# Gated linear attention and a gated expert on one core: smaller tiles on TensorE, decays loaded once, and new constants for the planner

## The chip, the cores and the metric

The kernel runs on one core of one Trainium2 chip. The time is the device time of one execution in microseconds (us); three executions of the kernel before were timed, and one more was profiled.

## The reference

For each of 4 batches and 8 heads, a state of 48 x 48 numbers is carried over 768 steps; its result, reshaped to 3072 tokens of 384 values, goes through a normalised, gated expert. All is float32.

```python
B, H, S, D = 4, 8, 768, 48
for t in range(S):
    state = alpha[:, :, t, :, None] * state + einsum('bhd,bhe->bhde', k[:, :, t], v[:, :, t])
    y[:, :, t] = einsum('bhd,bhde->bhe', q[:, :, t], state)
x  = y as (3072, 384)
xn = x / sqrt(mean(x * x) + 1e-6) * rms_g
g, val = xn @ w_gate, xn @ w_val            # (384, 1536) each
out = (g * sigmoid(g) * val) @ w_out        # (1536, 384)
```

## The kernel before

**Chunks.** The sequence is cut into 24 chunks of 128 steps (6 per batch; c0 to c3 are the first chunk of each batch, c4 to c7 the second, and so on). Eight heads make four pairs: the two heads of a pair lie on partitions 0 to 47 and 64 to 111. Products are kept near float32 by writing each operand as a high and a low f16 half and adding three products (`SPLIT`): high x high, high x low, low x high.

**Attention of a chunk** (`attention`, one operation after the other): SyncE (SP) loads `att`, 112 rows that hold four segments of decays (back half turned, front half, back half, front half turned), then q and k. VectorE (DVE) runs one scan over two segments (`scan`, L601), takes reciprocals of its ends into `seed2` (`turn`, L606), runs a second scan over the other two, and multiplies k and q by the products of decays (`mul_k` L616, `mul_q` L621). Both scans write in place, over the decays in `att`. ScalarE (ACT) copies the ends of the first scan into `dec` (`ends`, L609). Then come f16 halves of k, q and v (ACT the high, DVE the low), the scores on TensorE (PE) (`scores`, L691), the mask (L704), f16 halves of the masked scores (L755, L758), and the output `y` (`output`). For each pair of heads `output` makes six matmuls of q with the state (L772: stationary 48 x 128, 48 moving columns) and six of the scores with v (L781: stationary 128 x 128, 48 moving columns). `sums` (L798: stationary 64 x 64 or 64 x 48, 48 moving columns, 48 matmuls a chunk) renews the state. For c0 to c3 scores and output are float32 matmuls (L699, L731). After that the norm makes `x16` (L850, L854, L857), and a transposing DMA writes it to `xT`.

**Expert.** The chunks form groups of 4, 2, 2, 4, 4, 4, 4. For each group, `expert_in` makes for 12 blocks f of the hidden size two sets of nine matmuls (L982) of 512 or 256 columns, then `silu` (L993), `gate` (L999), the high f16 half (L478) and the low one (L1012); `expert_out` makes the output matmuls (L1052). On PE the expert matmuls are chained in a fixed order: group 0 in, group 0 out, group 1 in, and so on; attention is placed between them. In group 0 the first `EARLY` = 3 blocks f are run on two chunks at a time (256 columns), the others on four.

**Weights.** 18 blocks (i0 to i11, o0 to o5) are loaded as 64-bit words and decoded by DVE: `shift` L520, `sign` L523, `rest` L528, and a low half (`low`, L536). For the names in `LOW_W` PE and ACT make the low half instead: an identity matmul in float32 (`bring`, L541), one that subtracts the high half (`less`, L548), and a copy by ACT (`residue`, L554).

**Order.** All operations go to a planner (`Plan.order`). Each has a cost, a due time worked back from its group's planned time (`PACE`, `GAP`, `AHEAD`, `STRIDE`, `FIRST_DUE`), and a shift by kind (`LATE`). The planner plays the engines through in time and, among operations that could start, takes the one that is due first; the instructions are then written to each engine in that order, and each engine runs them in that order whatever happens. `BUFS` says how many buffers a name has; `att` has three.

**Verdict.** At the end `verdict` squares and sums statistics and sets a flag that picks a slow general path if a value was out of bounds. One matmul there (L1188) sums 411 columns over the partitions, and DVE adds them up (L1190).

Of the kernel before, what the change touches and what calls it, by code (L numbers as in the profile page):

```python
# [8 lines left out]
F32 = mybir.dt.float32  # L9
# [3 lines left out]
ALU = mybir.AluOpType  # L13
# [15 lines left out]
SPLIT = ((0, 0), (0, 1), (1, 0))  # L29
# [12 lines left out]


GROUPS = [4, 2, 2, 4, 4, 4, 4]
EARLY = 3


OUT32 = 4
LOW_A = ()
LOW_H = ()  # L50
LOW_W = ("i0", "i1", "i2", "i3")

BUFS = dict(
    att=3, v=2, kh=2, qp=2, k16=2, q16=2, kT=2, v16=4, gd=2, a16=2, ss=2, x32=1, x16=2,
    xT=2, raw=2, wu=2, h16=13, sl=2, h32=3, ob=2, at=3, y=1, mm=3,
)

# [4 lines left out]
    abs=0.92, wh=0.83, pow=0.65, sc=0.8, sc32=2.3, y=0.87, y0=0.5, y32=1.85, u=0.45, po=1.48,  # L62
    neg=0.3, wid=1.6, wneg=0.45, wl2=0.85,
)
IN_COST = {
# [4 lines left out]
LOAD_LAG, LOAD_END, LOAD_RATE = 0.6, 0.9, 230.0  # L70


PACE = [1.0, 1.0, 1.15, 1.18, 1.18, 1.18, 1.18]
GAP = [0, 14, 0, 0, 0, 0, 0]
FIRST_DUE = [-14.0, -8.0, -2.0, 4.0]
AHEAD = [0, 4, 8, 12, 16, 16, 16]
STRIDE = [0, 8, 12, 12, 20, 20, 20]
LATE = dict(load=0.0)
CUTS = [0, 2, 4]
SIDE = [3, 1]  # L80

# [1 line left out]
class Plan:  # L83
# [6 lines left out]
        self.users = {}  # L90
        self.slot = {}

    def op(self, engine, cost, fn, deps=(), use=(), due=None, lock=False, kb=0, late=0.0):

        o = dict(e=engine, c=cost, fn=fn, d=[d for d in deps if d], u=tuple(use), due=due, lock=lock,
                 kb=kb, late=late, i=len(self.ops), n=[])
        for d in o["d"]:
            d["n"].append(o)
        for k in o["u"]:
            self.users[k] = self.users.get(k, 0) + 1  # L100
        self.ops.append(o)
        return o

    def order(self):
# [8 lines left out]
        engine = dict.fromkeys(("PE", "DVE", "ACT", "POOL", "SP"), 0.0)  # L113
        ready = {e: [] for e in engine}
        wait = {o["i"]: len(o["d"]) for o in self.ops}
        for o in self.ops:
            o["r"] = 0.0
            if not o["d"]:
                ready[o["e"]].append(o)
        bus, port, done = 0.0, 0.0, []  # L120
# [209 lines left out]
def tile_attn_moe(  # L330
# [42 lines left out]
    raw_in = {}  # L373
    HC = C // 2
    SEG = NP * (HC + 1)
    o_a = 2 * SEG
    o_q = 4 * SEG
    o_k = o_q + NP * C

    def src(cc):  # L380
# [108 lines left out]
    def add(engine, kind, *args, **kw):  # L489
        return op(engine, COST[kind], *args, late=LATE.get(kind, 0.0), **kw)  # L490

    def decode(src, dst, name, col):
# [63 lines left out]
            )  # L556

        raw, wu = ("raw", name), ("wu", name)
        o = op("SP", 0.9, load, [], [raw], kb=786, late=LATE["load"])
# [20 lines left out]
    def attention(cc, due):  # L580
# [6 lines left out]
        def key(tag):  # L587
            return tag, cc
# [4 lines left out]
        def by_half(x):  # L593
            return x.rearrange("r p (g c) -> r g p c", g=2)

        def wseg():
            return att_tile(cc)[:, :o_q].rearrange("r (g p c) -> r g p c", g=4, p=NP)

        def scan(lo, start):
            x = att_tile(cc)[:, lo : lo + o_a]  # L600
            nc.vector.tensor_tensor_scan(  # L601
                x, x, start.rearrange("r g p c -> r (g p c)"), 0.0, op0=ALU.mult, op1=ALU.add
            )

        def turn():
            nc.vector.reciprocal(seed2[:, :, :, 0:1], wseg()[:, 2:4, :, HC : HC + 1])  # L606

        def ends():
            nc.scalar.copy(dec[:, cc], wseg()[:, 2:4, :, HC])  # L609
# [3 lines left out]
        def mul_k():  # L613
            t["kh"] = tl(ap, [R, NP, C], F32, "kh")
            k = att_tile(cc)[:, o_k:].rearrange(halves, p=NP, g=2)
            nc.vector.tensor_tensor(by_half(t["kh"]), k, wseg()[:, 0:4:3, :, :HC], op=ALU.mult)  # L616

        def mul_q():
            t["qp"] = tl(ap, [R, NP, C], F32, "qp")
            q = att_tile(cc)[:, o_q:o_k].rearrange(halves, p=NP, g=2)  # L620
            nc.vector.tensor_tensor(by_half(t["qp"]), q, wseg()[:, 1:3, :, 1:], op=ALU.mult)  # L621

        def k_hi():
            t["k16"] = tl(ap, [R, 2, NP, C], F16, "k16")
# [34 lines left out]
        def decay():  # L659

            t["gd"] = tl(ap, [R, NP, 1], F32, "gd")
            nc.vector.scalar_tensor_tensor(
                t["gd"][:, :, 0],
                dec[:, cc, 1],
                S_QP / (S_Q[1] * S_K[0]) * S_T / (S_K[1] * S_V),
                dec[:, cc - NB, 0],
                op0=ALU.mult,
                op1=ALU.mult,
            )
# [81 lines left out]
        def a_tile():  # L751
            return tile_of(("a16", cc), lambda: tl(ap, [P, 2, 2, NP, C], F16, "a16"))
# [9 lines left out]
        def output(h):  # L762
            if h == 0:
                t["y"] = tl(ps_y, [P, 2, 512], F32, "y")
            yps = t["y"]
            for p in (2 * h, 2 * h + 1):
                cs = slice(p * D, (p + 1) * D)
                if not first:
                    for m, (x, y) in enumerate(SPLIT):
                        for j in range(2):  # L770
                            r = slice(64 * j, 64 * j + D)
                            nc.tensor.matmul(  # L772
                                yps[:, j, cs],
                                t["q16"][r, x, p, :],
                                states[b][2][r, y, p, :],
                                start=m == 0,
                                stop=False,
                            )
                for j in range(2):
                    for m, (x, y) in enumerate(SPLIT):  # L780
                        nc.tensor.matmul(  # L781
                            yps[:, j, cs],
                            a_tile()[:, j, x, p, :],
                            t["v16"][:, y, j, p, :],
                            start=first and m == 0,
                            stop=m == 2,
                        )
# [78 lines left out]
        def x_turn():  # L866
# [4 lines left out]
                transpose=True,  # L871
            )

        att_k, at0, at1 = key("att"), ("at", (cc, 0)), ("at", (cc, 1))
        cuts = ((o_a, o_q), (0, o_a), (o_q, AW)) if cc < 2 else ((0, AW),)
        la = [
            op("SP", 0.45, lambda lo=lo, hi=hi: load_att(cc, lo, hi), use=[att_k], kb=(hi - lo) * R / 250)
            for lo, hi in cuts
        ]
        lv = op("SP", 0.45, lambda: load_v(cc), use=[key("v")], kb=196)  # L880
# [4 lines left out]
        s1 = add("DVE", "scan", lambda: scan(o_a, seed), [la[0]], [att_k], lock=True)  # L885
        rec = add("DVE", "rec", turn, [s1, prev.get("s2")], [att_k])
        de = add("ACT", "dec", ends, [s1], [att_k])
        s2 = add("DVE", "scan", lambda: scan(0, seed2), [rec, la[1 % len(la)]], [att_k], lock=True)
        kh = add("DVE", "kh", mul_k, [s2, la[-1]], [att_k, key("kh")], lock=True)
        qp = add("DVE", "kh", mul_q, [s2, la[-1]], [att_k, key("qp")], lock=True)  # L890
# [248 lines left out]
    def verdict():  # L1139
# [5 lines left out]
        def piece(rows, n):  # L1145
            used[0] += n
            return work[:rows, used[0] - n : used[0]]

        ones, sq, ok = piece(P, 1), piece(P, NS), piece(P, nok)
# [40 lines left out]
        nc.vector.tensor_reduce(  # L1190
            tot[:, 0:1], pok, axis=mybir.AxisListType.X, op=ALU.add
        )
        nc.vector.tensor_scalar(
            tot[:, 1:2],
            tot[:, 0:1],
# [35 lines left out]
def layout(inputs):  # L1231
# [8 lines left out]
    def pairs(x, pad):  # L1240
# [58 lines left out]
```

## Time and profile before

| | us |
|---|---|
| timed, median of 3 | 560.13 |
| timed, lowest and highest | 559.03, 560.67 |
| profiled execution | 559.45 |
| its span | 557.7 |
| PE busy in the span | 522.6 |
| DVE busy | 402.9 |
| ACT busy | 237.6 |

The profiled execution lies 0.68 us below the median and takes 1.75 us more than its span. Busy time is the time in which an engine had an instruction running. Matmuls overlap, so a busy PE may still do its work faster or slower; for a run of matmuls the distance from its first start to the start of what follows says more than the durations. The engines work at different loads in different stretches, so the shares over the whole span say little about what one change is worth.

### The profile page before, as it was taken

The page shows a single profiled execution, that of the slowest core. Times are in us where ns is not written, and L with a number is a line of the kernel's source. Part 1 is how long each engine was busy: PE and PEld are TensorE (multiplying, and loading weights), DVE is VectorE, ACT ScalarE, POOL GpSimd, SP SyncE. Part 2 cuts the span into 40 slices and gives each one's busy share as a digit, 9 for nine tenths or more (in the row PEclk, how much of TensorE's full clock was granted, in tenths as well). Part 3 has the DMA queues.
Part 4 walks back from the last instruction along what each step waited for, and adds up shares of the span by engine and source line. Part 5 has one row for each costly group of instructions (what it writes and reads, how often), then busy time and mean ns, then how long its engine had stood idle before and what let it go on. Part 6 is the DMA issues. An engine that isn't in the chain of part 4 may idle for free.

```text
span 557.7 us, 12089 instructions
## 1 busy us (share of the span) xinstructions
PE 522.6 (94%) x4986; PEld 309.0 (55%) x4986; DVE 402.9 (72%) x727; ACT 237.6 (43%) x636; POOL 22.1 (4%) x53
## 2 busy tenths in 40 slices
PE   2878899898999999999999999999999999999995
PEld 1756644355786787554556555456554456544452
DVE  7999999999996999787785687784577642133303
ACT  2446666755343665255542345542356431132300
POOL 2001000001000000000000010000000000000000
PEclk9986999989999999999999999999999999999998
DMA  8997875563822872334235233332211001000001
GB/s 221 298 303 151 259 199 168 170 179 62 222 68 48 176 176 70 72 90 102 48 81 128 75 82 99 46 82 61 74 29 18 15 15 45 28 1 0 1 29 34
DMA packets 59695, 56.15 MB, mean 101 GB/s; under 512 B 39472, under 2 KB 54960, under 8 KB 57168
## 3 DMA queue, kind: packets, MB, share of 16 engines
q1 hardware_dynamic: 59632, 55.30, 38.7%
q8 instruction: 41, 0.67, 0.5%
q14 instruction: 22, 0.18, 0.1%
HBM read 41.26 MB, written 4.72 MB: 82 GB/s over the span
## 4 chain that ended last, share of the span: by engine, by line
PE 79%; DVE 14%; DMA 4%; issue 2%; ACT 1%; SPq 0%; DVEq 0%
PE mm L982 47%; PE mm_po L1052 22%; PE y L781 3%; PE at L691 2%; PE y L772 2%; DMA rg<-rms_g 2%; DVE att L601 1%; PE at L798 1%; DVE wu_i L523 1%; DVE wu_o L523 1%; DVE wu_o L528 1%; DMA att<-att 1%; DMA kT<-k 1%; DVE wo L536 1%; DVE h L1012 1%
## 5 line engine op out<-in xcount | busy, mean ns | idle before, releaser
L982 PE MATMUL mm<-xT,wg 128*128 128x512 f16 (+1 forms) x1566 | 290.2, 344 | 3.4 <-ACT sl L993 1.6
L982 PEld LDWEIGHTS <-wg 128*128 128x128 f16 x1566 | 151.3, 98 | 127.1 <-issue 3.1
L1052 PE MATMUL mm_po<-wo,h 128*128 128x384 f16 x864 | 147.1, 328 | 5.8 <-DVE h L999 2.7
L1052 PEld LDWEIGHTS <-h 128*128 128x128 f16 x864 | 83.5, 98 | 63.0 <-issue 9.8
L478 ACT ACTIVATE h<-h 128x512 f16<-128x512 f32 (+1 forms) x87 | 48.2, 554 | 86.5 <-DVE h L999 86.0
L999 DVE SCALAR_TENSOR_TENSOR h<-mm,sl 128x512 f32<-128x512 f32 (+1 forms) x87 | 51.5, 592 | 41.6 <-PE mm L982 41.6
L1012 DVE TENSOR_TENSOR h<-h,h 128x512 f16<-128x512 f32 (+1 forms) x87 | 51.3, 591 | 20.9 <-ACT h L478 20.9
L601 DVE TENSOR_TENSOR_SCAN att<-att,seed 112x520 f32<-112x520 f32 x48 | 59.2, 1235 | 6.6 <-DMA att<-att 6.0
L993 ACT ACTIVATE sl<-mm 128x512 f32<-128x512 f32 (+1 forms) x87 | 45.1, 518 | 40.6 <-PE mm L982 40.0
L1063 DVE TENSOR_SCALAR ob<-mm_po 128x384 f32<-128x384 f32 x24 | 13.1, 551 | 33.4 <-PE mm_po L1052 33.3
L846 POOL TENSOR_TENSOR ss<-ss,mhalf 128x1 f32<-128x1 f32 x24 | 17.8, 740 | 444.4 <-DVE ss L836 408.7
L755 ACT CAST a<-at 128x512 f16<-128x512 f32 x40 | 23.2, 585 | 17.6 <-DVE at L704 17.4
L704 DVE TENSOR_TENSOR at<-at,mask 128x512 f32<-128x512 f32 x40 | 26.1, 692 | 4.1 <-PE at L691 4.0
L758 DVE TENSOR_TENSOR a<-at,a 128x512 f16<-128x512 f32 x40 | 25.9, 682 | 0.4
L781 PE MATMUL y<-v,a 128*128 128x48 f16 x480 | 25.7, 185 | 0.0
L830 ACT ACTIVATE junk<-y 128x384 bf16<-128x384 f32 x24 | 11.8, 490 | 31.0 <-DVE x L850 17.4
L478 ACT ACTIVATE v<-v 128x384 f16<-128x384 f32 x24 | 12.5, 519 | 26.2 <-PE at L798 23.9
L628 DVE TENSOR_TENSOR k<-kh,k 112x512 f16<-112x512 f32 x24 | 16.5, 686 | 9.6 <-ACT k L478 9.6
L478 ACT ACTIVATE k<-kh 112x512 f16<-112x512 f32 x24 | 15.0, 626 | 14.4 <-DMA kT<-k 9.9
L850 DVE TENSOR_TENSOR x<-y,rg 128x384 f32<-128x384 f32 x24 | 13.2, 552 | 9.9 <-PE y L781 8.4
L854 ACT ACTIVATE x<-x,ss 128x384 f16<-128x384 f32 x24 | 14.7, 611 | 13.4 <-POOL ss L846 12.6
L772 PE MATMUL y<-s,q 48*128 48x48 f16 x480 | 19.7, 184 | 0.0
(99 smaller groups left out, 426.7 us busy)
## 6 DMA issues: line engine op xcount, KB each, us to landing
att<-att SPq DMA_DIRECT2D x22, 903.0 KB, 5.8
v<-vtok SPq DMA_DIRECT2D x24, 192.0 KB, 2.8
raw_i<-w_gate SPq DMA_DIRECT2D x12, 384.0 KB, 4.0
raw_i<-w_val SPq DMA_DIRECT2D x12, 384.0 KB, 4.8
raw_o<-w_out SPq DMA_DIRECT2D x6, 768.0 KB, 4.5
out_dram<-ob SPq DMA_DIRECT2D x24, 192.0 KB, 2.1
att<-att SPq DMA_DIRECT2D x4, 227.5 KB, 4.1
att<-att SPq DMA_DIRECT2D x2, 448.0 KB, 7.4
```

The costliest lines, as they stand in the source:

```text
L478: nc.scalar.activation(dst, src, AF.Copy, scale=scale, accum_out=stat[:rows, col : col + 1])
L601: nc.vector.tensor_tensor_scan(x, x, start.rearrange("r g p c -> r (g p c)"), 0.0, op0=ALU.mult, op1=ALU.add)
L704: nc.vector.tensor_tensor(t["sc"][j], t["sc"][j], mask[:, int(first)].to_broadcast([P, NP, C]), op=ALU.mult,)
L755: nc.scalar.copy(a_tile()[:, j, 0], t["sc"][j])
L758: nc.vector.tensor_tensor(a_tile()[:, j, 1], t["sc"][j], a_tile()[:, j, 0], op=ALU.subtract)
L772: nc.tensor.matmul(yps[:, j, cs], t["q16"][r, x, p, :], states[b][2][r, y, p, :], start=m == 0, stop=False,)
L781: nc.tensor.matmul(yps[:, j, cs], a_tile()[:, j, x, p, :], t["v16"][:, y, j, p, :], start=first and m == 0, stop=m == 2,)
L982: nc.tensor.matmul(ps[:, :n], wg[:, f, x, j, kk, :], xT[:, y, kk, cs], start=i == 0, stop=i == 3 * NK - 1,)
L993: nc.scalar.activation(t["sl"][:, :n], t[0][:, :n], AF.Silu, scale=1.0 / (S_X * S_W))
L999: nc.vector.scalar_tensor_tensor(t["h"][:, :n], t[1][:, :n], S_H / (S_X * S_W), t["sl"][:, :n], op0=ALU.mult, op1=ALU.mult,)
L1012: nc.vector.tensor_tensor(h16_of(g, f)[:, 1, cs], t["h"][:, :n], h16_of(g, f)[:, 0, cs], op=ALU.subtract)
L1052: nc.tensor.matmul(t[i][:, :DM], h16_of(g, f)[:, x, ts], wo[:, f // 2, y, f % 2, :], start=f == 0 and m == 0, stop=f == NF - 1 and m == 2,)
```

## The change

- `att` now holds the decays once: back half, then front half reversed in time and in pair order, with one column more. The row falls from 2064 to 1545 numbers. The first scan reads the segment forward, the second reads the same numbers backward (a step of -1), and both write into a new tile `dk`, which has a single buffer. The reciprocals, `mul_k`, `mul_q` and `decay` read it with the pairs in reverse where needed. For c0 and c1 the load is cut in two parts and not three.
- `output` cuts each matmul in two: L772's into four tiles of 48 x 64 (two heads, two halves of the queries), L781's into two of 128 x 64. A chunk after c3 has 96 matmuls there and not 48. Columns, products and sums are the same.
- `verdict` adds along the columns on DVE first, and its last matmul has one column.
- `EARLY` is 5, `LOW_W` is i0, i1, o1, i11, i7.
- All constants of the planner's due times are new, `LATE` has an entry for most kinds, and `HOLD` gives times in the plan before which the loads of some chunks and weights are not taken. `HOLD` changes the order only; the engine does not wait for a time.

```diff
-EARLY = 3
+EARLY = 5
-LOW_W = ("i0", "i1", "i2", "i3")
+LOW_W = ['i0', 'i1', 'o1', 'i11', 'i7']
-    att=3, v=2, kh=2, qp=2, k16=2, q16=2, kT=2, v16=4, gd=2, a16=2, ss=2, x32=1, x16=2,
+    att=3, v=2, kh=2, qp=2, k16=2, q16=2, kT=2, v16=4, gd=2, a16=2, ss=2, dk=1, x32=1, x16=2,
-PACE = [1.0, 1.0, 1.15, 1.18, 1.18, 1.18, 1.18]
-GAP = [0, 14, 0, 0, 0, 0, 0]
-FIRST_DUE = [-14.0, -8.0, -2.0, 4.0]
-AHEAD = [0, 4, 8, 12, 16, 16, 16]
-STRIDE = [0, 8, 12, 12, 20, 20, 20]
-LATE = dict(load=0.0)
+PACE = [0.939, 1.309, 1.366, 1.325, 1.11, 1.095, 1.217, 1.519]
+GAP = [0, 9.2, -0.3, -0.8, 7.1, 0.3, 11.3, 10.4]
+FIRST_DUE = [-19.3, -19.1, -6.2, -12.5]
+AHEAD = [0, 6.1, 6.5, 12.3, 23.9, 15.3, 13.6, 8.2]
+STRIDE = [0, 4.9, 9.6, 16.8, 26.0, 20.7, 39.7, 9.1]
+LATE = dict(
+    abs=-14.0, al=-0.2, gd=2.4, h=-10.0, hl=5.8, k16=12.3, kl=1.0, load=6.5, mask=0.9,
+    neg=-4.7, ob=-12.5, po=17.9, q16=4.2, ql=1.2, rec=-4.0, rest=0.6, sc=-10.0, scan=2.8,
+    sd=1.5, shift=-3.4, sign=-6.0, sl=3.9, sq=2.0, ss=-4.6, st=-8.0, u=-15.4, v16=14.9,
+    vl=-8.0, wh=8.0, wid=3.9, wl=1.9, wneg=-15.1, x=-5.9, x16=12.4, xl=-4.5, y=-3.4,
+)
+HOLD = dict(
+    c10=51.1, c11=64.8, c2=1.0, c5=9.2, c6=12.0, c7=38.1, c8=98.8, i1=19.5, i10=43.3,
+    i11=21.3, i4=33.0, i5=48.0, i6=24.5, i9=26.4, o1=68.1, o3=36.2,
+)
...
-    o_a = 2 * SEG
-    o_q = 4 * SEG
+    o_q = 2 * SEG + 1
...
-        def scan(lo, start):
-            x = att_tile(cc)[:, lo : lo + o_a]
+        def scan(turned):
+            if not turned:
+                t["dk"] = tl(ap, [R, 4 * SEG], F32, "dk")
+            x = att_tile(cc)
+            x = x[:, o_q - 1 : 0 : -1] if turned else x[:, : o_q - 1]
+            out = t["dk"][:, : 2 * SEG] if turned else t["dk"][:, 2 * SEG :]
+            start = seed2 if turned else seed
             nc.vector.tensor_tensor_scan(
-                x, x, start.rearrange("r g p c -> r (g p c)"), 0.0, op0=ALU.mult, op1=ALU.add
+                out, x, start.rearrange("r g p c -> r (g p c)"), 0.0, op0=ALU.mult, op1=ALU.add
             )
...
-            nc.vector.tensor_tensor(by_half(t["kh"]), k, wseg()[:, 0:4:3, :, :HC], op=ALU.mult)
+            nc.vector.tensor_tensor(by_half(t["kh"]), k, wseg()[:, 1:4:2, ::-1, :HC], op=ALU.mult)
...
-                if not first:
-                    for m, (x, y) in enumerate(SPLIT):
+                for m, (x, y) in enumerate(() if first else SPLIT):
+                    for n in range(2):
+                        rows = slice(n * HC, (n + 1) * HC)
                         for j in range(2):
                             r = slice(64 * j, 64 * j + D)
                             nc.tensor.matmul(
-                                yps[:, j, cs],
-                                t["q16"][r, x, p, :],
+                                yps[rows, j, cs],
+                                t["q16"][r, x, p, rows],
...
-                for j in range(2):
-                    for m, (x, y) in enumerate(SPLIT):
-                        nc.tensor.matmul(
-                            yps[:, j, cs],
-                            a_tile()[:, j, x, p, :],
+                for m, (x, y) in enumerate(SPLIT):
+                    for j in (1, 0):
+                        for rows in (slice(HC, P), slice(0, HC)):
+                            nc.tensor.matmul(
+                                yps[rows, j, cs],
+                                a_tile()[:, j, x, p, rows],
...
-        cuts = ((o_a, o_q), (0, o_a), (o_q, AW)) if cc < 2 else ((0, AW),)
+        cuts = ((0, o_q), (o_q, AW)) if cc < 2 else ((0, AW),)
...
+        nc.vector.tensor_reduce(all_ok, ok, axis=mybir.AxisListType.X, op=ALU.add)
         yield
-        pok = buf(ps_at, [1, nok], F32, "at", "pok")
-        nc.tensor.matmul(pok, ones, ok, start=True, stop=True)
+        pok = buf(ps_at, [1, 1], F32, "at", "pok")
+        nc.tensor.matmul(pok, ones, all_ok, start=True, stop=True)
```

## Rows read from the trace of the kernel before

**Rows 1.** Page, busy time of each engine: us, share of span, instructions.

```profile
PE 522.6 (94%) x4986; PEld 309.0 (55%) x4986; DVE 402.9 (72%) x727; ACT 237.6 (43%) x636; POOL 22.1 (4%) x53
```

**Rows 2.** Stages: length, busy us of each engine, PE clock, DMA share, GB/s.

```profile
4.00:47.83 43.83, 28.37 (x236) 23.46 (x237) 42.25 (x67) 18.47 (x52) 3.53 (x8) 0.90 0.94 251
47.83:133.90 86.07, 77.57 (x639) 43.92 (x639) 84.98 (x135) 53.98 (x140) 3.26 (x8) 0.95 0.67 186
133.90:226.00 92.10, 91.35 (x1199) 70.90 (x1199) 83.99 (x176) 46.69 (x150) 3.62 (x6) 1.00 0.51 121
226.00:551.40 325.40, 325.32 (x2916) 170.71 (x2914) 190.54 (x349) 116.99 (x294) 8.47 (x12) 1.00 0.22 52
```

**Rows 3.** Chain that ended last, around 133 us: start, us, what.

```profile
132.98 0.88 DVE wo L536
133.90 2.92 PE mm_po L1052 x17
...
144.41 23.58 PE mm L982 x216
```

**Rows 4.** Timeline of PE over one chunk's sums and output: start, us.

```profile
122.41 0.56 PE L798 MATMUL at<-v,kT 64*64 64x48 f16 x48
122.90 0.25 PE L772 MATMUL y<-s,q 48*128 48x48 f16 x6
123.08 0.32 PE L781 MATMUL y<-v,a 128*128 128x48 f16 x6
123.33 0.25 PE L772 MATMUL y<-s,q 48*128 48x48 f16 x6
...
124.54 3.25 PE L1052 MATMUL mm_po<-wo,h 128*128 128x384 f16 x19
```

**Rows 5.** Groups of PE from 133.9 us on: busy us, mean ns.

```profile
L772 PE MATMUL y<-s,q 48*128 48x48 f16 x432 | 17.7, 184 | 0.0
```

**Rows 6.** Timeline of PE over the verdict's matmuls.

```profile
544.02 0.46 PE L1161 MATMUL at_pst<-raw_work 128*1 128x177 f32 x2
544.41 4.56 PE L1052 MATMUL mm_po<-wo,h 128*128 128x384 f16 x27
548.90 0.85 PE L1188 MATMUL at_pok<-raw_work 128*1 128x411 f32 x2
549.69 1.64 PE L1052 MATMUL mm_po<-wo,h 128*128 128x384 f16 x9
```

**Rows 7.** Groups of DVE up to 133.9 us: busy us, mean ns, idle before.

```profile
L601 DVE TENSOR_TENSOR_SCAN att<-att,seed 112x520 f32<-112x520 f32 x16 | 19.7, 1236 | 2.7 <-DMA att<-att 2.4
...
L536 DVE TENSOR_TENSOR wg<-wu_i,wg 128x768 f16<-128x768 f32 x8 | 7.6, 945 | 0.0
...
L616 DVE TENSOR_TENSOR kh<-att 112x512 f32<-112x512 f32 x7 | 4.8, 682 | 0.1
...
L606 DVE RECIPROCAL seed<-att 112x8 f32<-112x8 f32 x8 | 1.6, 203 | 0.3
```

**Rows 8.** Groups of DVE over the span, shapes apart.

```profile
L999 DVE SCALAR_TENSOR_TENSOR h<-mm,sl 128x512 f32<-128x512 f32 x57 | 39.2, 687 | 40.5 <-PE mm L982 40.5
...
L999 DVE SCALAR_TENSOR_TENSOR h<-mm,sl 128x256 f32<-128x256 f32 x30 | 12.4, 412 | 1.0 <-PE mm L982 1.0
```

**Rows 9.** Timeline of PE over the low half of a weight.

```profile
59.03 1.46 PE L541 MATMUL y_i<-wu_i,same 128*128 128x384 f32 x4
60.32 0.49 PE L548 MATMUL y_i<-wg,minus 128*128 128x384 f16 x2
60.74 0.84 PE L691 MATMUL at<-q,k 48*128 48x128 f16 x24
```

**Rows 10.** Timeline of DVE, first and last of ten scans after 140 us.

```profile
140.81 1.23 DVE L601 TENSOR_TENSOR_SCAN att<-att,seed 112x520 f32<-112x520 f32 x1
...
163.74 1.24 DVE L601 TENSOR_TENSOR_SCAN att<-att,seed 112x520 f32<-112x520 f32 x1
```

**Rows 11.** DMA issues: KB each, median us to landing.

```profile
att<-att SPq DMA_DIRECT2D x22, 903.0 KB, 5.8
```

More of the change, by code (lines that the diff above doesn't have):

```diff
@@ L44 @@
 GROUPS = [4, 2, 2, 4, 4, 4, 4]
-EARLY = 3
+EARLY = 5
 OUT32 = 4
-LOW_A = ()
-LOW_H = ()
-LOW_W = ("i0", "i1", "i2", "i3")
+LOW_A = []
+LOW_H = []
+LOW_W = ['i0', 'i1', 'o1', 'i11', 'i7']
 BUFS = dict(
-    att=3, v=2, kh=2, qp=2, k16=2, q16=2, kT=2, v16=4, gd=2, a16=2, ss=2, x32=1, x16=2,
+    att=3, v=2, kh=2, qp=2, k16=2, q16=2, kT=2, v16=4, gd=2, a16=2, ss=2, dk=1, x32=1, x16=2,
     xT=2, raw=2, wu=2, h16=13, sl=2, h32=3, ob=2, at=3, y=1, mm=3,
@@ L61 @@
     dec=0.1, k16=0.62, v16=0.52, q16=0.62, s16=0.26, a16=0.5, sq=0.58, x16=0.53, st0=0.22,
-    abs=0.92, wh=0.83, pow=0.65, sc=0.8, sc32=2.3, y=0.87, y0=0.5, y32=1.85, u=0.45, po=1.48,
+    abs=0.92, wh=0.83, pow=0.65, sc=0.8, sc32=2.3, y=0.78, y0=0.5, y32=1.85, u=0.45, po=1.48,
     neg=0.3, wid=1.6, wneg=0.45, wl2=0.85,
@@ L91, in __init__, with op @@
         self.slot = {}
-    def op(self, engine, cost, fn, deps=(), use=(), due=None, lock=False, kb=0, late=0.0):
+    def op(self, engine, cost, fn, deps=(), use=(), due=None, lock=False, kb=0, late=0.0, hold=0.0):
         o = dict(e=engine, c=cost, fn=fn, d=[d for d in deps if d], u=tuple(use), due=due, lock=lock,
-                 kb=kb, late=late, i=len(self.ops), n=[])
+                 kb=kb, late=late, r=hold, i=len(self.ops), n=[])
         for d in o["d"]:
@@ L116, in order @@
         for o in self.ops:
-            o["r"] = 0.0
             if not o["d"]:
@@ L558, in decode @@
         raw, wu = ("raw", name), ("wu", name)
-        o = op("SP", 0.9, load, [], [raw], kb=786, late=LATE["load"])
+        o = op("SP", 0.9, load, [], [raw], kb=786, late=LATE["load"], hold=HOLD.get(name, 0.0))
         o = add("ACT", "abs", fold, [o], [raw, wu])
@@ L596, in wseg @@
         def wseg():
-            return att_tile(cc)[:, :o_q].rearrange("r (g p c) -> r g p c", g=4, p=NP)
-        def scan(lo, start):
-            x = att_tile(cc)[:, lo : lo + o_a]
+            return t["dk"].rearrange("r (g p c) -> r g p c", g=4, p=NP)
+        def scan(turned):
[5 more added lines that the diff above has]
+            start = seed2 if turned else seed
             nc.vector.tensor_tensor_scan(
-                x, x, start.rearrange("r g p c -> r (g p c)"), 0.0, op0=ALU.mult, op1=ALU.add
+                out, x, start.rearrange("r g p c -> r (g p c)"), 0.0, op0=ALU.mult, op1=ALU.add
             )
         def turn():
-            nc.vector.reciprocal(seed2[:, :, :, 0:1], wseg()[:, 2:4, :, HC : HC + 1])
+            nc.vector.reciprocal(
+                seed2.rearrange("r g p c -> r (g p) c")[:, ::-1, 0],
+                wseg()[:, 2:4, :, HC].rearrange("r g p -> r (g p)"),
+            )
         def ends():
@@ L620, in mul_q @@
             q = att_tile(cc)[:, o_q:o_k].rearrange(halves, p=NP, g=2)
-            nc.vector.tensor_tensor(by_half(t["qp"]), q, wseg()[:, 1:3, :, 1:], op=ALU.mult)
+            nc.vector.tensor_tensor(by_half(t["qp"]), q, wseg()[:, 0:4:2, :, 1:], op=ALU.mult)
         def k_hi():
@@ L663, in decay @@
                 t["gd"][:, :, 0],
-                dec[:, cc, 1],
+                dec[:, cc, 1, ::-1],
                 S_QP / (S_Q[1] * S_K[0]) * S_T / (S_K[1] * S_V),
@@ L778, in output @@
                             )
-                for j in range(2):
-                    for m, (x, y) in enumerate(SPLIT):
-                        nc.tensor.matmul(
-                            yps[:, j, cs],
-                            a_tile()[:, j, x, p, :],
[L784 to L787, printed above, removed]
+                for m, (x, y) in enumerate(SPLIT):
[4 more added lines that the diff above has]
+                                a_tile()[:, j, x, p, rows],
+                                t["v16"][:, y, j, p, :],
+                                start=first and m == 0,
+                                stop=m == 2,
+                            )
         def sums():
@@ L872, in x_turn @@
             )
+        dk = key("dk")
         att_k, at0, at1 = key("att"), ("at", (cc, 0)), ("at", (cc, 1))
-        cuts = ((o_a, o_q), (0, o_a), (o_q, AW)) if cc < 2 else ((0, AW),)
+        cuts = ((0, o_q), (o_q, AW)) if cc < 2 else ((0, AW),)
         la = [
-            op("SP", 0.45, lambda lo=lo, hi=hi: load_att(cc, lo, hi), use=[att_k], kb=(hi - lo) * R / 250)
+            op("SP", 0.45, lambda lo=lo, hi=hi: load_att(cc, lo, hi), use=[att_k], kb=(hi - lo) * R / 250, hold=HOLD.get(f"c{cc}", 0.0))
             for lo, hi in cuts
@@ L884, in attention @@
         prev = state_ops.get(cc - 1, {})
[L885 to L890, printed above, removed]
+        s1 = add("DVE", "scan", lambda: scan(False), [la[0]], [att_k, dk], lock=True)
+        rec = add("DVE", "rec", turn, [s1, prev.get("s2")], [dk])
+        de = add("ACT", "dec", ends, [s1], [dk])
+        s2 = add("DVE", "scan", lambda: scan(True), [rec], [att_k, dk], lock=True)
+        kh = add("DVE", "kh", mul_k, [s2, la[-1]], [att_k, dk, key("kh")], lock=True)
+        qp = add("DVE", "kh", mul_q, [s2, la[-1]], [att_k, dk, key("qp")], lock=True)
         kd = add("ACT", "k16", k_hi, [kh], [key("kh"), key("k16")])
@@ L1147, in piece @@
             return work[:rows, used[0] - n : used[0]]
-        ones, sq, ok = piece(P, 1), piece(P, NS), piece(P, nok)
+        ones, sq, ok, all_ok = piece(P, 1), piece(P, NS), piece(P, nok), piece(P, 1)
         thr, row, tot = piece(1, NS), piece(1, NS), piece(1, 2)
@@ L1185, in verdict @@
             )
+        nc.vector.tensor_reduce(all_ok, ok, axis=mybir.AxisListType.X, op=ALU.add)
         yield
-        pok = buf(ps_at, [1, nok], F32, "at", "pok")
-        nc.tensor.matmul(pok, ones, ok, start=True, stop=True)
+        pok = buf(ps_at, [1, 1], F32, "at", "pok")
+        nc.tensor.matmul(pok, ones, all_ok, start=True, stop=True)
         yield
-        nc.vector.tensor_reduce(
-            tot[:, 0:1], pok, axis=mybir.AxisListType.X, op=ALU.add
-        )
+        nc.vector.tensor_copy(tot[:, 0:1], pok)
         nc.vector.tensor_scalar(
@@ L1210, in tile_attn_moe @@
     v = op("PE", 0.2, lambda: next(it), [v], [work, pst], due=now - 7)
-    v = op("DVE", 3.0, lambda: next(it), [v], [work, pst], due=now - 4)
-    v = op("PE", 0.5, lambda: next(it), [v], [work, pok], due=now - 3)
-    v = op("DVE", 1.0, lambda: next(it, None), [v], [work, pok], due=now - 2)
+    v = op("DVE", 3.5, lambda: next(it), [v], [work, pst], due=now - 4)
+    v = op("PE", 0.1, lambda: next(it), [v], [work, pok], due=now - 3)
+    v = op("DVE", 0.5, lambda: next(it, None), [v], [work, pok], due=now - 2)
     with tc.manual_schedule():
@@ L1253, in layout @@
     parts = [
-        np.concatenate([zero, x], axis=3) for x in (back[..., ::-1], front, back, front[..., ::-1])
-    ] + [pairs(q.reshape(cut), 0), pairs(k.reshape(cut)[:, :, :, ::-1], 0)]
+        np.concatenate([zero, x], axis=3) for x in (back, front[:, :, ::-1, ::-1])
+    ] + [zero[:, :, :1]] + [pairs(q.reshape(cut), 0), pairs(k.reshape(cut)[:, :, :, ::-1], 0)]
     att = np.concatenate([x.reshape(B * n, 112, -1) for x in parts], axis=2)
```

## The prediction, made before the changed kernel ran

> **What bounds the kernel now.** I read the page's busy times first. PE is busy for 522.6 of 557.7 us and DVE for 402.9 [rows 1], which points to PE but hides that the span has two parts. So I cut the span into stages. From 226 us on PE has work for 325.32 of 325.40 us, and from 133.9 to 226 for 91.35 of 92.10: there each microsecond that PE saves ends the kernel that much earlier. Before 133.9 it is DVE: it works 42.25 + 84.98 = 127.23 of the 129.90 us from 4 us on (98%), while PE waits, and its mean clock is 0.90 and 0.95 of full [rows 2]. The chain of waits says the same: it runs over DVE up to the low half of the last weight at 133.86, and from there on over PE alone; group 1's expert matmuls begin at 144.41 [rows 3]. So two questions decide: when does DVE release PE, and how much work has PE left then?
>
> **Output in smaller tiles.** In the row of one chunk, six L772 start at 122.90, six L781 at 123.08, the next six L772 at 123.33, and the chunk's output is over at 124.54 [rows 4]. So a pair takes 0.18 + 0.25 us and a chunk 124.54 - 122.90 = 1.64, of which 4 x 0.18 = 0.72 is for the state and 0.92 for the scores. What does a quarter cost? The nearest row is `sums`, which has the same 48 moving columns and runs in four quarters of the array, as the new state part will: 48 matmuls from 122.41 to 122.90, so 0.49 / 48 = 10.2 ns each and 41 ns for a round of four [rows 4]. At that pace the state's 48 new matmuls take 48 x 10.2 ns = 0.49 us, 0.23 less.
>
> The scores' 48 new ones use two tiles (halves of the queries) with all 128 rows. No row has that form, so I bound it. Below: 10.2 ns each, 0.49 us (0.43 less). Above: the halves don't run side by side, and each takes the 41 ns that a tile takes for one load and one matmul in `sums`: 48 x 41 = 1.97 us (1.05 more). I take 41 ns for a pair of halves, since a tile can't turn round faster than it does in `sums` unless issue alone sets that: 24 x 41 ns = 0.98, 0.06 more. Sum 1.47 us a chunk, 0.17 less. 432 of the 480 L772 lie behind 133.9 us, which is 18 chunks [rows 5]: **-3.1 us**, between -18 x 0.66 = -11.9 and +18 x 0.82 = +14.8. The two chunks before that save nothing, as DVE covers them.
>
> A rule of the Trainium skill speaks against this edit: "TensorEngine Tiling (Array Packing)", section Performance Considerations (Instruction Overhead), gives each matmul some 60 cycles whatever its columns, and warns against tiling a dimension that is small already; here the moving columns are 48. At 2.4 GHz that is an estimate of 25 ns for each of the 96, so 2.4 us a chunk, 0.76 more than now and +13.7 us in all. The rows disagree with it at 10.2 ns a matmul where four tiles alternate [rows 4]; for two tiles no row here shows it. The same page, section Restrictions, says that column tiling switches Fast Weight Load off; that would be the upper bound's mechanism.
>
> **Verdict.** Its last matmul holds PE from 548.90 to 549.69, 0.79 us; the other one, of 177 columns, takes 544.41 - 544.02 = 0.39 [rows 6]. With one column it takes less than that; I take 0.25, so **-0.5 us** (between -0.4 and -0.8). The added reduction runs on DVE, which is 59% busy from 226 us on [rows 2].
>
> **Weights and EARLY, on DVE before 133.9.** A fifth name in `LOW_W` takes one low half of 0.95 us from DVE [rows 7], so **-0.95**. In its place PE gets 60.74 - 59.03 = 1.71 us [rows 9] and ACT a copy; PE waits in that stretch anyway, and if a block falls behind the release it costs the 1.71 instead. Two more blocks run in halves: gate takes 2 x 0.41 us there and not 0.69 [rows 8], 0.14 more, and the low half, of the same shapes, I cost alike: 0.14 x 2 operations x 2 blocks = 0.54. Instructions in a row overlap at their ends, so I take **+0.4**. The half-width matmuls cost PE a little more too; that is under the same cover.
>
> **Decays once.** The two scans keep their 520 columns each, so I put their cost at nothing gained. The second reads backward, which no row shows. The scan takes 1236 ns for 520 columns, 2.4 ns each, and a product of two tensors 682 ns for 512, 1.3 ns each [rows 7]; the recurrence is slower than reading, so I take 0. Above: were it to take another scan's time, 1.24 us x 6 chunks = +7.4 us before the release. The load falls from 903 KB to some 676 KB a chunk; its landing of 5.8 us [rows 11] is hidden already, since DVE waited 2.7 us for loads in the whole first part, 2.4 of it at the first scan [rows 7], whose piece keeps its size: 0. `dk` has one buffer. Behind a waiting first scan stands all of DVE, since the next chunk must wait for ACT's copy of the ends and for both products of the chunk before. The trace runs ten scans ahead between 140.81 and 163.74 [rows 10]; the new kernel can be ahead by two chunks only, as `kh` and `qp` have two buffers. That costs while DVE is short of time: from 133.9 to 226 it has 92.10 - 83.99 = 8.1 us free [rows 2], which covers it.
>
> **The order.** This is the large unknown. Up to 133.9 DVE ran 16 scans, eight chunks' worth, and seven multiplications by k [rows 7], but groups 0 and 1, which PE needs first, have six chunks. So 4 scans (4.9 us), two reciprocals (0.4) and three products of one chunk (2.0), 7.3 us in all, were for group 2 and stood ahead of the last weights. DVE's own idle time there is 2.7 us [rows 2]. If all of it goes, the release comes 10.0 us earlier. What is moved must be done before group 2 begins, and the 8.1 us free up to 226 take it. The new constants push that way: `shift` and `sign` are due 3.4 and 6 us earlier, scans 2.8 later, and group 1 is stretched by 1.309, so that group 2 is due later. I take two thirds, **-6.7 us**, between 0 and -10.0.
>
> Sum: -3.1 - 0.5 - 0.95 + 0.4 - 6.7 = -10.85, so 559.45 - 10.85 = 548.6 for a profiled execution. The one here lies 0.68 us under the median of three (560.13), so **549.3 us** for the median.
>
> **Rivals.**
> *A, the halves don't run side by side.* Place: L781, behind the release. For: no row has a tile of 128 x 64, and rows 4 show side-by-side work only where the tiles differ in rows too. Against: a round of four in 41 ns would hardly fit if two of the four took turns. Price +14.8 in place of -3.1: 549.3 + 17.9 = 567 us, slower. It decides from this point: all else gives 7.75 us, or 0.43 a chunk over 18; with 0.23 from the state part, L781 may grow from 0.92 to 1.58 us, 66 ns for a pair of halves. Beyond that the kernel is slower. The Trainium skill's page named above, with both of its rules, speaks for this rival.
>
> *B, the order brings nothing.* The plan works with costs, not with what the queues do, and each engine must keep the order. For: the plan of before had costs near the rows as well and still ran group 2 early. Then 549.3 + 6.7 = 556 us, faster still by a little.
>
> *C, the order stalls PE.* With scans only two chunks ahead, a group's first chunk comes late. If the 8.1 us free up to 226 don't come in time, PE waits for them: 556 + 8.1 = 564 us. Against: the present plan had PE wait 0.75 us there.
>
> *D, everything is recovered.* The release comes 10.0 us earlier and a pair of halves takes 20 ns: 549.3 - 3.3 - 8.8 = 537 us.
>
> **How the numbers follow.** Three timed runs span 1.6 us, 0.3%: a smaller difference can't be told from none (558.5 to 561.8). Chances: my forecast (543 to 554) 0.55; B 0.15, of which 0.04 is within 0.3%; D 0.10; A 0.11, of which 0.02 stays within 0.3% since the halves may be only partly in turn; C 0.09. So faster 0.55 + 0.11 + 0.10 = 0.76, the same 0.06, slower 0.09 + 0.09 = 0.18. The range runs from 539, inside D, to 562, which holds B and the mild ends of A and C; I leave out some 0.2: half of D, most of A, half of C.
>
> **What would show it.** In the changed profile: the output of a chunk at 1.47 us from its first L772 to what follows (A would show over 2.0); scans at 1.24 us both ways; the last low half of a weight finished near 127, and group 1's matmuls some 7 us before 144.4; fewer than 16 scans ahead of the last weight; PE without waits behind it; the verdict's last matmul at a quarter of a microsecond. The prediction is wrong if the release stays at 134 or PE waits at the start of groups 2 or 3, if the backward scan is slower, or if PE has more work behind the release because weights' low halves ended up there.

## The result: 0.34% slower, where 1.9% faster was forecast

The changed kernel takes 561.81 us (median of 20 runs, 559.45 to 563.18), the kernel before 559.72 (20 runs); the ratio is 1.0034, interval [1.0025, 1.0043]. The forecast was 549.3, from 539 to 562.

The page's busy times of the changed kernel (span 560.6 us):

```profile
PE 532.4 (95%) x5988; PEld 322.6 (58%) x5988; DVE 400.4 (71%) x731; ACT 238.4 (43%) x643; POOL 25.1 (4%) x53
```

PE is busy 10 us longer than in [rows 1], DVE 2.5 us less. The stages, cut where the changed kernel's own events lie (length, busy us of PE, PEld, DVE, ACT, POOL, PE clock, DMA share, GB/s), first up to the last low half of a weight, then from there on:

```profile
4.00:127.14 123.14, 105.89 (x902) 72.36 (x902) 118.07 (x187) 71.10 (x188) 6.71 (x15) 0.93 0.72 191
```

```profile
127.14:138.27 11.13, 11.13 (x175) 6.99 (x167) 10.64 (x23) 3.78 (x12) 0.96 (x2) 1.00 0.74 174
138.27:226.00 87.73, 87.73 (x1588) 69.83 (x1584) 83.52 (x177) 48.16 (x153) 5.58 (x6) 1.00 0.44 103
226.00:553.63 327.63, 327.61 (x3352) 173.43 (x3340) 186.92 (x343) 113.87 (x288) 8.72 (x12) 1.00 0.20 47
```

DVE's timeline with the last low half of a weight; the chain that ended last, around the start of group 1 (start, us, what); and PE's timeline at its last wait before that, with the wait in brackets:

```profile
126.18 0.95 DVE L544 TENSOR_TENSOR wo<-wu_o,wo 128x768 f16<-128x768 f32 x1
```

```profile
131.60 5.96 PE mm_po L1073 x36
137.56 0.78 PE at L709 x24
138.34 15.83 PE mm L1003 x144
```

```profile
118.13 0.31 PE L801 MATMUL y<-v,a 128*64 128x48 f16 x8 [0.92 <-DVE v L664]
```

Set beside [rows 2, 3]: DVE's last weight is done at 127.13 instead of 133.86, and group 1 begins at 138.34 instead of 144.41, 6.1 us earlier. That weight no longer holds PE: PE's last wait for DVE ends at 118.13, for a low half of v, and from there on PE has next to no idle time. So the first part gained nearly what was forecast, and the second part lost more. PE's timeline shows where, in a chunk's output:

```profile
125.97 0.28 PE L791 MATMUL y<-s,q 48*64 48x48 f16 x12
126.18 0.37 PE L801 MATMUL y<-v,a 128*64 128x48 f16 x12
126.48 0.28 PE L791 MATMUL y<-s,q 48*64 48x48 f16 x12
...
127.71 0.37 PE L801 MATMUL y<-v,a 128*64 128x48 f16 x12
128.02 0.50 PE L1073 MATMUL mm_po<-wo,h 128*128 128x384 f16 x2
```

A pair of heads takes 0.21 us for the state and 0.30 for the scores, a chunk 128.02 - 125.97 = 2.05 us; in [rows 4] it was 1.64. The verdict's last matmul is now short:

```profile
551.86 0.19 PE L1210 MATMUL at_pok<-raw_work 128*1 128x1 f32 x2
551.98 1.64 PE L1073 MATMUL mm_po<-wo,h 128*128 128x384 f16 x9
```

The sum, row by row: from group 1's first matmul to the end of PE's last one passed 551.33 - 144.41 = 406.9 us before and 553.62 - 138.34 = 415.3 after, 8.4 more. Behind that point lie 18 chunk outputs of 2.05 us now (864 matmuls in the next row) and lay 17 of 1.64 before, since c6's came ahead of it: 36.9 - 27.9 = +9.0; the verdict gives back 0.79 - 0.12 = 0.67, which makes 8.3 of the 8.4. Two smaller terms cancel: PE's idle time of 0.75 us between 133.9 and 226 [rows 2] is gone, and the new order writes the two halves of eight chunks apart, so that PE comes from another tile shape into the output 26 times and not 18, at some 0.1 us each (experiment 3). With -6.1 at the start and +0.6 at the tail (6.98 us behind PE's last matmul, 6.37 before) the span grows by 2.9, as measured.

```profile
L791 PE MATMUL y<-s,q x864: 186/186/207, 154.9 to 473.5; 48*64 48x48 f16 x173
```

### The profile page after: what moved, and what is told of

The parts are those of the page before. It is cut to its first block, busy times and chain, and to the rows that moved or that the text cites. A ratio compares the mean times of both kernels' runs of the same rounds, so it can differ in the third digit from the quotient of the medians.

```text
span 560.6 us, 14125 instructions
## 1 busy us (share of the span) xinstructions
PE 532.4 (95%) x5988; PEld 322.6 (58%) x5988; DVE 400.4 (71%) x731; ACT 238.4 (43%) x643; POOL 25.1 (4%) x53
## 4 chain that ended last, share of the span: by engine, by line
PE 83%; DVE 11%; issue 2%; DMA 2%; SPq 0%; ACT 0%; DVEq 0%; ACTq 0%
PE mm L1003 45%; PE mm_po L1073 24%; PE y L801 4%; PE y L791 3%; PE at L709 3%; DMA att<-att 2%; PE at L818 1%; DVE wu_i L531 1%; DVE dk L616 1%; PE y L749 1%; DVE h L1020 1%; PE y_i L549 1%; DVE h L1033 1%; DVE wu_i L528 1%; DVE wu_o L531 1%
## 5 line engine op out<-in xcount | busy, mean ns | idle before, releaser
L1003 PEld LDWEIGHTS <-wg 128*128 128x128 f16 x1602 | 154.5, 99 | 120.9 <-issue 0.7
L616 DVE TENSOR_TENSOR_SCAN dk<-att,seed 112x520 f32<-112x520 f32 x48 | 59.4, 1237 | 3.0 <-DMA att<-att 2.2
L866 POOL TENSOR_TENSOR ss<-ss,mhalf 128x1 f32<-128x1 f32 x24 | 20.8, 866 | 383.8 <-DVE ss L856 352.3
L801 PE MATMUL y<-v,a 128*64 128x48 f16 x960 | 29.9, 193 | 0.9 <-DVE v L664 0.9
L870 DVE TENSOR_TENSOR x<-y,rg 128x384 f32<-128x384 f32 x24 | 13.3, 555 | 21.1 <-PE y L801 16.5
L801 PEld LDWEIGHTS <-a 128*64 128x64 f16 x960 | 21.5, 111 | 3.7 <-issue 1.0
L717 PE MATMUL at<-qp,kh 48*128 48x128 f32 x64 | 8.6, 428 | 14.7 <-DVE qp L639 11.9
L791 PE MATMUL y<-s,q 48*64 48x48 f16 x960 | 22.4, 193 | 0.0
L791 PEld LDWEIGHTS <-q 48*64 48x64 f16 x960 | 14.1, 106 | 10.9 <-issue 8.6
```

Source lines behind the costliest of these rows:

```text
L616: nc.vector.tensor_tensor_scan(out, x, start.rearrange("r g p c -> r (g p c)"), 0.0, op0=ALU.mult, op1=ALU.add)
L791: nc.tensor.matmul(yps[rows, j, cs], t["q16"][r, x, p, rows], states[b][2][r, y, p, :], start=m == 0, stop=False,)
L801: nc.tensor.matmul(yps[rows, j, cs], a_tile()[:, j, x, p, rows], t["v16"][:, y, j, p, :], start=first and m == 0, stop=m == 2,)
L1003: nc.tensor.matmul(ps[:, :n], wg[:, f, x, j, kk, :], xT[:, y, kk, cs], start=i == 0, stop=i == 3 * NK - 1,)
```

## The experiments

**1. The output's tiles, put back and made alone.** `full_tiles` is the changed kernel with `output` as it was; `tiles_alone` is the kernel before with only the new `output`.

```diff
 # full_tiles, against the changed kernel
-                                yps[rows, j, cs],
-                                t["q16"][r, x, p, rows],
+                                yps[:, j, cs],
+                                t["q16"][r, x, p, :],
...
-                    for j in (1, 0):
-                        for rows in (slice(HC, P), slice(0, HC)):
...
```

> The changed kernel with the output in full tiles as before; all else stays changed. Theory 1 (the smaller tiles cost 0.51 us a pair against 0.43, on a PE that has no slack behind 138 us, and all else gained): a chunk falls from 2.05 to 1.64 us, 18 chunks give 7.4 us, two more lie where PE has little slack and give up to 0.8, so 561.8 - 7.4 to 8.2 = 553.6 to 554.4, 1.0% below the kernel before. Rival (the new order or dk costs the time, and the output's tiles are only where it shows): PE waits elsewhere, and the time stays above 558.

> The kernel before with only the output cut into smaller tiles. Theory 1: 18 chunks behind the release at 133.9 us at 0.41 us each, +7.4 us (567.1); the two before it are covered by DVE. Rival (a chunk's output costs 2.05 us only in the new order, where it is put between other matmuls): 559.7 to 562.

Measured: 551.9 us (0.9857 of the kernel before, [0.9843, 0.9872]) and 570.25 (1.0176, [1.0153, 1.0198]). The tiles cost the changed kernel 9.9 us and the kernel before 10.3, more than the 7.4 to 8.2 that the rows give. In `full_tiles` 1.8 us of it lie ahead of group 1, which begins at 136.56 there and not at 138.34; in `tiles_alone` PE also waits once more, 1.95 us at 189.66, whose cause no row shows. All else in the change is worth 8.0 us.

**2. Quarters for the state alone.** The state part as in the change, the scores part in full tiles.

```diff
-                for m, (x, y) in enumerate(SPLIT):
-                    for j in (1, 0):
-                        for rows in (slice(HC, P), slice(0, HC)):
+                for j in range(2):
+                    for m, (x, y) in enumerate(SPLIT):
...
```

> The changed kernel with the state part in quarters and the scores part in full tiles. By the rows of the two profiles a pair takes 0.205 (quarters) + 0.255 (full) = 0.46 us against 0.43 and 0.51, so 0.03 x 4 x 18 = 2.2 us above the version with full tiles, about 556. Theory 2 (a change of tile shape costs a fixed time, and the quarters themselves run at the 10 ns of the sums): the state part takes 0.2 again. Rival (quarters are slower because of what they alternate with, half tiles): 0.12 us for the state part, and 3 us below the version with full tiles.

Measured: 555.51 us (0.9921, [0.9906, 0.9936]), 3.6 above full tiles where 2.2 was expected. The state part alone loses too, although `sums` runs quarters at 10.2 ns each; halves of the scores have the other 6.3 us.

**3. Fewer and more changes of tile shape.** `turned_full` has full tiles and makes, for the two pairs of a half chunk, scores, state, state, scores instead of state, scores, state, scores; `turned_alone` puts that order into the kernel before, `turned_small` into the changed kernel's small tiles. `more_changes` has full tiles and takes turns after every two matmuls.

```diff
 # turned_*: p is a pair, two pairs in a half chunk
+                late = not first and p == 2 * h
...
+                for part in (of_scores, of_state) if late else (of_state, of_scores):
+                    part()
...
 # more_changes, against full_tiles: the scores' loop moves into the state's loop over m
-                for j in range(2):
-                    for m, (x, y) in enumerate(SPLIT):
+                    for j in range(2):
                         nc.tensor.matmul(
                             yps[:, j, cs],
                             a_tile()[:, j, x, p, :],
...
```

> The changed kernel with full tiles and another order inside the output: of the two pairs of a half chunk the first does scores then state, the second state then scores, so that the tile shape changes twice for each half chunk (expert's shape, state's, expert's) and not four times; matmuls, their number and their shapes stay those of the kernel before. Theory 2 (each change of shape costs about 0.1 us: with 48 matmuls of the sums in 0.49 us and 12 of the quarters in 0.205, a pace of 7.9 ns and a fixed 0.11 us fit both): 4 changes fewer a chunk give 0.4 us, a chunk takes 1.2 us, 18 chunks give 7.2 us below the version with full tiles, about 546.5. Rival (loading small tiles sets the pace and a change costs nothing): no difference to the version with full tiles, 553.6 to 554.4.

> The kernel before with only the order inside the output changed (scores, state, state, scores of the two pairs of a half chunk). Theory 2: 4 changes of tile shape fewer a chunk, 0.42 us, for 18 chunks behind the release: -7.5 us, 552.4. Rival (the gain needs the new order around it): 556 to 560.

> The changed kernel with its small tiles, but scores, state, state, scores inside a half chunk. Each of its parts has a shape of its own, so a half chunk has five changes of shape now and four then (expert's shape at both ends). Theory 2: one change fewer for each half, 0.1 us, 0.2 a chunk, 18 to 20 chunks: 3.6 to 4.2 us below the changed kernel's 561.8, 558; it stays some 13 us above the same order in full tiles (545.1), since full tiles of the scores have the expert's shape. Rival (a change costs nothing with small tiles): 561.8.

> The changed kernel with full tiles, and for each pair of heads state and scores taken in turn three times (two matmuls of the state, two of the scores, and so on) and not six and six: the same 48 matmuls a chunk with the same shapes and 16 changes of tile shape more. Theory 2 (0.09 to 0.11 us for each change, the time between the last and the first matmul of two shapes beyond their pace): 16 x 0.1 = 1.6 to 1.7 us a chunk, 18 to 20 chunks, so 29 to 34 us above the 551.9 of the version with full tiles: 581 to 586. Rival (the cost of small tiles is loading them, a change is free): 552.

Measured: `turned_full` **545.13 us** (0.9735, [0.9722, 0.9747]), 6.8 below full tiles; `turned_alone` 553.72 (0.99, [0.9886, 0.9915]); `turned_small` 556.61 (0.9935, [0.9917, 0.9953]), 5.2 below the changed kernel where 3.6 to 4.2 was expected; `more_changes` 597.48 (1.0676, [1.0661, 1.0692]). In each pair of kernels the matmuls, their shapes and their number are the same; how often the shape changes differs, and with it the order. `turned_small` gained more than expected since in ten of its eighteen chunks the two halves stand together: there three changes go, not two. PE's timeline of one chunk in `full_tiles` (its last pair) and in `turned_full`:

```profile
266.45 0.25 PE L790 MATMUL y<-s,q 48*128 48x48 f16 x6
266.63 0.32 PE L799 MATMUL y<-v,a 128*128 128x48 f16 x6
266.79 1.46 PE L1001 MATMUL mm<-xT,wg 128*128 128x512 f16 x6
```

```profile
262.48 0.31 PE L803 MATMUL y<-v,a 128*128 128x48 f16 x6
262.72 0.32 PE L792 MATMUL y<-s,q 48*128 48x48 f16 x12
262.98 0.47 PE L803 MATMUL y<-v,a 128*128 128x48 f16 x12
263.38 0.32 PE L792 MATMUL y<-s,q 48*128 48x48 f16 x12
263.63 0.32 PE L803 MATMUL y<-v,a 128*128 128x48 f16 x6
263.80 2.53 PE L1008 MATMUL mm<-xT,wg 128*128 128x512 f16 x11
```

Six scores matmuls take 0.16 to 0.17 us when an expert matmul of the same 128 x 128 shape follows, and 0.24 to 0.25 when the state's 48 x 128 follow: a change costs 0.08 to 0.09. Six more state matmuls in a row add 0.26 - 0.18 = 0.08 us, 13 ns each, which leaves 0.10 of the 0.18 for the change. Small tiles show the same in `turned_small`:

```profile
267.05 0.37 PE L806 MATMUL y<-v,a 128*64 128x48 f16 x12
267.35 0.38 PE L794 MATMUL y<-s,q 48*64 48x48 f16 x24
267.66 0.56 PE L806 MATMUL y<-v,a 128*64 128x48 f16 x24
268.15 0.38 PE L794 MATMUL y<-s,q 48*64 48x48 f16 x24
```

24 quarters take 0.31 us where 12 took 0.21: 8 ns each and 0.11 fixed. 24 halves take 0.49 where 12 took 0.30: 16 ns each, 32 a pair, and 0.11 fixed. That the shape counts, and not another operand or output, `sums` shows in the changed kernel. Its 48 matmuls run in quarters too; they take 0.40 us where the state's quarters follow, about 48 x 8 ns, and 0.49 where the expert's full tiles follow:

```profile
116.37 0.56 PE L818 MATMUL at<-v,kT 64*64 64x48 f16 x48
116.77 0.27 PE L791 MATMUL y<-s,q 48*64 48x48 f16 x12
```

```profile
131.04 0.56 PE L818 MATMUL at<-v,kT 64*64 64x48 f16 x48
131.53 6.02 PE L1073 MATMUL mm_po<-wo,h 128*128 128x384 f16 x36
```

`more_changes` missed its expectation: it lost 11.5 to 16.5 us more than its changes should cost. In its timeline a change costs what it should: four parts take 289.41 - 288.84 = 0.57 us, of which the paces above explain 4 x 0.013 + 4 x 0.025 = 0.15, so 0.10 for each change.

```profile
288.84 0.20 PE L789 MATMUL y<-s,q 48*128 48x48 f16 x2
288.97 0.22 PE L797 MATMUL y<-v,a 128*128 128x48 f16 x2
...
289.41 0.20 PE L789 MATMUL y<-s,q 48*128 48x48 f16 x2
```

But PE's clock falls. Its timeline at the start and the end of one chunk's output, and its stages (length, busy us of PE, PEld, DVE, ACT, POOL, PE clock, DMA share, GB/s):

```profile
260.91 0.20 PE L789 MATMUL y<-s,q 48*128 48x48 f16 x2
...
264.22 5.95 PE L999 MATMUL mm<-xT,wg 128*128 128x512 f16 x19
```

```profile
255.00:262.00 7.00, 7.00 (x45) 3.37 (x43) 6.96 (x12) 2.69 (x6) 0.00 (x0) 1.00 0.36 101
262.00:264.30 2.30, 2.30 (x35) 1.72 (x34) 0.62 (x2) 0.72 (x2) 0.00 (x0) 1.00 0.00 0
264.30:268.00 3.70, 3.70 (x13) 1.36 (x11) 2.06 (x4) 1.49 (x5) 0.55 (x1) 0.58 0.00 0
268.00:275.00 7.00, 7.00 (x79) 3.22 (x77) 2.96 (x6) 2.69 (x8) 0.00 (x0) 0.98 0.14 28
```

After the 3.3 us of such turns, from 260.91 to 264.22, the expert matmuls run for most of 3.7 us at 1.2 GHz and not 2.4 (mean 0.58 of full). From 138 to 480 us the clock's mean is 0.97 in this kernel and 1.00 in `full_tiles`, `turned_full` and `turned_small`; 0.03 of 342 us is an estimate of 10 us for it. The rest is open, and why the clock falls there is not shown.

**4. Order or data.** `order_alone`: the kernel before with the new planner constants, `HOLD`, `EARLY` and `LOW_W`, and with the planned cost of an output half that the changed kernel has (0.78 us for 0.87; the list of the change leaves it out). `decays_alone`: the kernel before with the decays loaded once, `dk`, and the new verdict. `same_order`: `full_tiles`' order with the old data; `one_slot`: `decays_alone`'s order with the old data (both give the planner a name `dk` with one slot that no tile uses, the sizes of the smaller loads, and two loads for three of c0 and c1; both have the new verdict).

```diff
 # order_alone, against the kernel before: the new constants, and
+        o = op("SP", 0.9, load, [], [raw], kb=786, late=LATE["load"], hold=HOLD.get(name, 0.0))
 # same_order, against full_tiles
-            x = x[:, o_q - 1 : 0 : -1] if turned else x[:, : o_q - 1]
+            x = att_tile(cc)[:, lo : lo + o_a]
...
-        np.concatenate([zero, x], axis=3) for x in (back, front[:, :, ::-1, ::-1])
+        np.concatenate([zero, x], axis=3) for x in (back[..., ::-1], front, back, front[..., ::-1])
```

> The kernel before with the planner's new constants, HOLD, EARLY = 5 and the new LOW_W; data, scans, output tiles and verdict stay. Theory 3 (the 8.0 us that the version with full tiles lies below the kernel before come from the order, of which DVE's earlier release is most): 552 to 553, group 1 begins some 6 us before 144.4. Rival (they come from loading the decays once, which frees DMA and a buffer): 558 to 560.

> The kernel before with the decays loaded once, the tile dk with one buffer, and the new verdict; the planner's constants, EARLY, LOW_W and the output's tiles are those of before. Theory 3: scans cost the same both ways, loads were hidden, so only the verdict's 0.5 us goes: 559.2 to 559.9. Rival 1 (fewer bytes matter): 555 or less. Rival 2 (one buffer for dk holds DVE up): over 561.

> The version with full tiles (551.9) with the data of before: four segments of decays in att, scans in place, loads of 903 KB. The planner is given the same operations, costs and buffers as there (a name dk with one slot, which no tile uses), so that it writes the same order. Theory 3 (the gain of 8 us lies in the order of the instructions, and bytes and scans are neutral): 551 to 553. Rival (the smaller loads give part of it): 555 to 560.

> The kernel before (its data, its planner's constants, full tiles) with the new verdict, in which only the plan is given the name dk with one slot: the order is that of decays_alone (577.6), the data that of before. Theory 4 (one slot changes the order that the old constants lead to, and that order costs 18 us): 576 to 579. Rival (reading decays backward or writing to another tile costs it on the chip): 559 to 561.

Measured: `order_alone` 561.49 us (1.0031, [1.0017, 1.0046]); `decays_alone` 577.58 (1.0317, [1.0303, 1.0331]); `same_order` 552.12 (0.9865, [0.9851, 0.9879]); `one_slot` 579.27 (1.0343, [1.033, 1.0356]). Both of the first two expectations missed: each half of the change alone is slower, the two together are 8 us faster. The last two runs say why. In each of them the instructions of PE, DVE, ACT and POOL stand in the order of its partner. With the same order, the old data gives 552.1 against 551.9, and 579.3 against 577.6: bytes, `dk` and the backward scan matter little, at most 1.7 us. The order is what counts, and the order comes from the constants and from what the planner is told of the new data (the slot, the sizes, the loads), together. Which of these three turns the order, no run tells: every run has all of them or none. When group 1 begins shows it, in `order_alone` and in `decays_alone`:

```profile
148.59 16.86 PE L990 MATMUL mm<-xT,wg 128*128 128x256 f16 x153
```

```profile
152.43 22.74 PE L993 MATMUL mm<-xT,wg 128*128 128x256 f16 x192
```

against 144.41 before, 138.34 in the changed kernel and 136.56 in `full_tiles`. In `decays_alone` that is 8.0 of the 18 us; behind it, up to 480 us, PE waits another 5.4 us (busy 322.17 of 327.57), and the clock's mean is 0.98 in place of 1.00. No run has a second slot for `dk`.

## Why the prediction was wrong, by its own steps

**What bounds the kernel** was right for the kernel before: DVE, then PE alone. In the changed kernel PE is alone from 118.13 on, and not only behind the last weight, so the chunk's output at 125.97, which the prediction took to be covered by DVE, counts as well.

**The order, weights and EARLY** (-6.7 - 0.95 + 0.4 = -7.25 us, or -7.75 with the verdict) came out near the forecast: DVE's last weight 6.7 us earlier, group 1 6.1, and 8.0 us in `full_tiles`. The mechanism holds, too: work for later groups went behind the last weight. Up to there DVE now works 118.07 us and not 127.2, with 14 scans instead of 16, five low halves of k (`kl`) instead of seven, and one low half of a weight less. This is the row of its scans up to 127.14 us:

```profile
L616 DVE TENSOR_TENSOR_SCAN dk<-att,seed 112x520 f32<-112x520 f32 x14 | 17.3, 1237 | 2.6 <-DMA att<-att 2.2
```

The close agreement is in part luck. The forecast took two thirds of 10.0 us, which were 7.3 us of moved work and all 2.7 us of DVE's idle time. In fact 9.1 us of work went, among it two of the four scans that it named and low halves that it did not, and 2.4 of that turned into more idle time (5.1 us, it had been 2.7). What the prediction did not see is that the constants do this only together with what the plan is told of the new data; it had put the one slot of `dk` down as a possible stall. Rivals B and C fall with that: the order gains, and PE does not wait at the start of a group.

**Decays once** at nothing was right: all 48 scans, forward and backward, take 1229 to 1243 ns, beside a mean of 1236 in [rows 7], and `same_order` lies within 0.2 us of `full_tiles`.

**The verdict** gave 0.67 us, forecast 0.5.

**The output in smaller tiles is the step that failed**: -3.1 us forecast, +9.9 measured. It took the pace of `sums`, 0.49 us / 48 = 10.2 ns, for a run of 48 matmuls, and applied it to runs of 12 between other shapes. In 0.49 us there is one change of tile shape; in the output there is one every 12 matmuls, of some 0.10 us each, which the sum put at nothing. The paces themselves were forecast too dear: 8 ns a quarter (10.2 forecast) and 32 ns a pair of halves (41). So the state part takes 0.84 us a chunk, 0.21 x 4, and not 0.49, and the scores 1.21 and not 0.98: 0.58 us a chunk missed, 10.4 us over 18 chunks, of the 13.0 between -3.1 and +9.9; 1.8 more lie ahead of group 1.

The tiles lose twice. By the paces alone a chunk's 96 small matmuls take 48 x 8 + 48 x 16 ns = 1.15 us, while the 48 full ones take 24 x 13 + 24 x 25 ns = 0.91; for a full tile of the scores (0.40 - 0.25) / 6 gives the 25 ns. And the halves of the scores no longer share the expert's shape, so a half chunk that stands alone has five changes and not four. Rival A named the right side, and by the prediction's own sign (over 2.0 us a chunk) it would have been taken for true; but its price needed 82 ns for a pair of halves, and a pair takes 32. How far the two halves run side by side, no row shows. The measured 561.8 lies within the range only at its upper end, which was left open for B, A and C.

The rule that bears on this was there: the Trainium skill, "TensorEngine Tiling (Array Packing)", section Tiling Modes (Key Properties), says that changing the tiling mode drains TensorE, while changing the tile does not. The trace agrees: 0.08 to 0.11 us at a change of shape, and none seen between `sums` and the state's quarters; that the engine drains there, no row shows. The rule of the same page of the Trainium skill that the prediction weighed, some 60 cycles for each matmul (section Performance Considerations, Instruction Overhead), the trace does not bear out for small tiles: 8 ns, against the prediction's estimate of 25.

## What to carry to other kernels

Read the pace of a small matmul from two lengths of run, not from one: the difference gives the pace, the rest is the price of changing the tile shape, and here that price (about 0.1 us) made up 0.73 of the output's 1.64 us before and 0.90 of its 2.05 after. Before cutting matmuls smaller, order them so that the shape changes less often; scores, state, state, scores brought 5 to 7 us in three kernels with the same matmuls, and with the new order and full tiles it makes the fastest kernel here, 545.1 us, 2.65% under the kernel before. Constants found for a planner belong to the buffers and loads that it was given: taken alone, either half of such a change can lose what both win.

## What the runs showed that was not expected

- What a planner is told (one slot, smaller loads, two loads for three) was worth 19 us with one set of constants (559.8 to 579.3), with the same data and all but the same instructions.
- Where the tile shape changed every two matmuls, the granted clock fell to a mean of 0.58 in the 3.7 us after a chunk's output, though PE was busy without a gap before and during it.
- A scan that reads with a step of -1 takes as long as one that reads forward: 1229 to 1243 ns for all 48.
